# The token product of the remainder rows in four quarters of the array instead of two halves

## The chip, the core and the metric

One NeuronCore of a Trainium2 chip runs the whole program. The metric is the device time of one execution in microseconds (us). A core has a matrix engine (TensorE, PE in the profile, with its weight loads listed as PEld), a vector engine (VectorE, DVE), a scalar engine (ScalarE, ACT), GpSimd (POOL), a queue for DMA issues (SyncE, SP) and 16 DMA engines. TensorE is an array of 128 rows by 128 columns: a weight block ("stationary", `lhsT`) is loaded into it, and a second operand ("moving", `rhs`) is streamed through. An instruction may use a part of the array only: the partitions of its operands choose the rows, the partitions of its output in PSUM choose the columns. A profile shows that as `64*128` (64 rows by 128 columns), `128*64` or `64*64`.

## The reference, cut to what matters

Attention without softmax, with an RMS norm, feeds an MLP mixer. All is fp32.

```python
kv = np.einsum('bhsd,bhse->bhde', k, v)
out = np.einsum('bhsd,bhde->bhse', q, kv)
x = out / rms * g_norm                      # (8, 8, 576, 64) -> x (8, 576, 512)
xt = x.transpose(0, 2, 1)
h = np.maximum(xt @ w_tok1, 0.0) @ w_tok2   # w_tok1 (576, 256), w_tok2 (256, 576)
u = x + h.transpose(0, 2, 1)
h2 = np.maximum(u @ w_ch1, 0.0) @ w_ch2     # w_ch1 (512, 1536), w_ch2 (1536, 512)
return u + h2
```

The change is in `xt @ w_tok1`, the first token product. Its sum runs over 576 sequence rows, four blocks of 128 and a remainder of 64.

## The kernel before, in words

The eight batches go in four pairs. For a pair, attention makes the rows x: `X[pair, c]` for c from 0 to 3 holds 128-row blocks, two each, the first four blocks for the pair's first batch and the next four for its second; `X[pair, 4]` holds the two remainders together, those of the first batch on partitions 0 to 63 and those of the second on 64 to 127 (`x_of(pair, 8)`). `w_tok1r` holds the 64 remainder rows of the token weights twice, on both partition halves. The weights come as 64-bit words that ACT and DVE decode into fp32: four ACT steps a block (lines 183 to 201), then three DVE steps (lines 204 to 213); this decoding of the channel weights runs beside the token mixing, one block after another.

Token mixing (`token_mixing`, line 611) has these steps for a pair:

- `h` followed by side and t (`tok1`, line 614): for each side (batch of the pair) and each half t of the 256 token channels, a sum over four 128-row blocks in a PSUM bank `acc[side, t]` of 128 partitions by 512. These use the whole array.
- `hr` (`tok1_rem`, line 621): the 64 remainder rows are added to all four banks. Side 0 uses array rows 0 to 63, side 1 rows 64 to 127; both have all 128 columns. Then four `relu` on ACT (line 130) copy the banks to `h1` in SBUF, which frees the banks.
- `z` (`seed`, line 632): ACT copies x into a PSUM bank ahead of a later product.
- `u0` to `u8` (`tok2`, line 638): the second token product, read from `h1`, in order; `u8` makes the remainder rows of both batches in two column halves of the array (`128*64`).

Attention has `kv` (line 399; from pair 1 on in column halves, `128*64`), `kr` (`kv_rem`, line 417; the remainder rows, in quarters, `64*64`) and, from pair 1 on, `a` (`attend`, line 465), also in quarters, with 64 moving columns.

Every instruction goes through a helper that keeps the program's order (`matmul` line 135, shown as L136; `relu` L130; `copy` L133; `tensor_add` L127; `dma` L124). The order is written by hand as lists of step names that `play` (line 1334) runs: `middle` (line 1398), the two lists of `steady` (line 1404) and `last` (line 1456). In `middle`, `hr` of pair 0 follows `kv01 kr0 e00 e01` of pair 1's attention and is followed by `a0`. In both lists of `steady`, `hr` (of pairs 1 and 2) follows `h11` and is followed by `a1` of the next pair's attention. In `last`, `hr` (of pair 3) follows `h11`, and `u0` comes next. On ACT, the four `relu` come after the decoding steps that the lists put ahead of `hr`, and ahead of the `z` copy.

PSUM has two banks tagged `o`, two `kv` and four `h` (line 97). `acc` takes the four `h` banks; the `z2` seed and then `u0` of pairs 0 to 2 take the first ones that the `relu` free. `u0` and `u1` of pair 3 take `o` banks.

After the four pairs come the channel products (`channel1_once` and on), from 182 us to the end: long runs of whole-array matmuls of 256 columns, with DVE sums around them.

Of the kernel before, what the change touches and what calls it, by code (L numbers as in the profile page):

```python
# [20 lines left out]
def kernel(  # L21
# [33 lines left out]
    P = 128  # L55
# [5 lines left out]
    J, JJ, HF, Q = 4, 5, 64, 32  # L61
# [41 lines left out]
    w_tok1r = tokw.tile([P, DTOK], F32, name="w_tok1r")  # L103
# [11 lines left out]
    def do(f, *a, **kw):  # L115
        return lambda: f(*a, **kw)
# [6 lines left out]
    def dma(o, i, engine=nc.sync):  # L123
        keep(engine.dma_start(o, i))  # L124

    def tensor_add(o, a, b, op=ALU.add, engine=nc.vector):
        keep(engine.tensor_tensor(out=o, in0=a, in1=b, op=op))  # L127

    def relu(o, a):
        keep(nc.scalar.activation(o, a, AF.Relu))  # L130

    def copy(o, a):
        keep(nc.scalar.copy(o, a))  # L133

    def matmul(*a, **kw):
        keep(nc.tensor.matmul(*a, **kw))  # L136
# [248 lines left out]
    def x_of(pair, i):  # L385

        return X[pair, i // 2][:, i % 2]
# [223 lines left out]
    def token_mixing(pair, seeds, aside=()):  # L611
        h1, acc = {}, {}

        def tok1(side, t, js=range(J)):
            if js[0] == 0:
                acc[side, t] = ps["h"].tile([P, DM], F32, name="ps_h", tag="h")
            for j in js:
                matmul(acc[side, t], lhsT=w_tok1[j // 2][:, j % 2, ts(t, P)],
                                 rhs=x_of(pair, side * J + j), start=(j == 0), stop=False)

        def tok1_rem():
            for t in range(NTOK):
                for side in range(2):
                    r = ds(side * HF, HF)
                    matmul(acc[side, t], lhsT=w_tok1r[r, ts(t, P)],
                                     rhs=x_of(pair, 8)[r], start=False, stop=True)
            for side in range(2):
                h1[side] = hp_.tile([P, NTOK, DM], F32, name="h1", tag="h1")
                for t in range(NTOK):
                    relu(h1[side][:, t], acc[side, t])  # L630

        def seed(i):


            acc[i] = ps["h"].tile([P, DM], F32, name="ps_u", tag="h")
            copy(acc[i], x_of(pair, i))

        def tok2(i):
            if i not in seeds:
                n = "o" if i in aside else "h"  # L640
                acc[i] = ps[n].tile([P, DM], F32, name="ps_u", tag=n)
            first = i not in seeds
            if i < 8:
                for t in range(NTOK):
                    matmul(acc[i], lhsT=w_tok2[:, t, ts(i % J, P)], rhs=h1[i // J][:, t],
                           start=(first and t == 0), stop=(t == NTOK - 1), skip_group_check=True)
            else:
                for t in range(NTOK):
                    for side in range(2):
                        matmul(acc[i][ds(side * HF, HF)], lhsT=w_tok2[:, t, LO:],  # L650
                               rhs=h1[side][:, t],
                               start=(first and t == 0), stop=(t == NTOK - 1), skip_group_check=True)
            x = x_of(pair, i)
            if first:
                tensor_add(x, acc[i], x)
            else:
                copy(x, acc[i])
            if i == 8:
                dma(u_rest[ts(pair, P)], x, nc.gpsimd)
                for side in range(2):  # L660
                    dma(out[2 * pair + side, LO:], x[ds(side * HF, HF)], nc.gpsimd)
            elif i % 2 == 1:
                dma(
                    u_rows(2 * pair + i // J)[ds((i % J - 1) * P, 2 * P)]
                    .rearrange("(t p) e -> p t e", p=P), X[pair, i // 2], nc.gpsimd)

        steps = {f"h{s}{t}": do(tok1, s, t) for s in range(2) for t in range(NTOK)}
        steps |= {f"h{s}{t}{j}": do(tok1, s, t, (j,)) for s in range(2) for t in range(NTOK) for j in range(J)}
        steps |= {f"z{i}": do(seed, i) for i in seeds}
        return steps | {"hr": tok1_rem} | {f"u{i}": do(tok2, i) for i in range(9)}  # L670
# [714 lines left out]
    def spread_g():  # L1385
# [5 lines left out]
    start = [  # L1391
        "j21 zk00 zk01 ka00 ka01 gs kb00 e00 kb01 e01 eg0 eg1 l0 w01 w02 w03 w04 j4",
        "a00 q00 t00 m00 r00 i00", "a01 q01", "ag dg g01 t01 m01", "a10 q10", "a11 q11 r01 zk10 zk11 i01 w51 d01 w52 w53 w54",
        "w30 w40 lq0 h000 h010", "kv10 e10 g10", "kv11 e11 g11 t10 t11 m1 r1 i1 d10 w11 w12 w13 w14 l1", "h001", "h011", "a20 q20",
        "a21 q21 s11", "a30 q30", "a31", "h002 h012 g20 g21 t20 t21 m2 r2 i2 d20 g30 q31 s21 g31 t30",
        "a40", "h003 h013 t31 m3",
        "r3 i3 d30 q40 s31 g40 t40 m4 r4 w21 i4 d40 lr0 lr1"]
# [161 lines left out]
```

## Time and profile before

| | us |
|---|---|
| time, median of 3 runs | 768.65 (768.58 to 768.66) |
| time of the profiled execution | 768.43 |
| its span, first to last instruction | 766.6 |
| PE busy in the span | 761.2 |
| matmuls of the remainder rows, 32 instructions, mean of one | 0.59 |
| PE waits in all, longest | 2.1, 1.1 |

The span leaves out what lies around the program's instructions. A busy PE is a PE with a matmul in its pipeline: matmuls overlap, and the profile lists a 512-column matmul at 0.59 us although the next begins 0.43 later. Two matmuls that use different parts of the array begin almost together, some 7 ns apart. "x8" in a timeline counts instructions; an fp32 matmul of the source is two of them, each with its weight load.

### The profile page before, as it was taken

What the parts mean: (1) busy time and instruction counts of PE and PEld (TensorE: products, weight loads), DVE (VectorE), ACT (ScalarE), POOL (GpSimd) and SP (SyncE); (2) the same over time, 40 slices, a digit from 0 to 9 for tenths busy, and PEclk for the clock granted to TensorE, in tenths of its full rate; (3) what the DMA queues carried; (4) which work ended last, traced back from release to release, by engine and by line L of the source; (5) the groups of instructions that cost most, each with busy time, mean ns of one, the idle gap of its engine ahead of it and who ended that gap; (6) DMA issues with size and microseconds to landing.
All of it is one profiled execution on the core that took longest, in us unless ns stands there. A gap on an engine that the chain in (4) does not pass through costs nothing.

```text
span 766.6 us, 12767 instructions
## 1 busy us (share of the span) xinstructions
PE 761.2 (99%) x4694; PEld 613.0 (80%) x4694; DVE 644.5 (84%) x958; ACT 279.0 (36%) x563; POOL 110.8 (14%) x121
## 2 busy tenths in 40 slices
PE   9999999999999999999999999999999999999998
PEld 8655555446888888888888888888888888888887
DVE  3868896997757779899969889997898996798997
ACT  3656575773210232511234242123352223325211
POOL 0003030203410000002240002042000218000204
PEclk9999999999999999999999999999999999999999
DMA  9999999799799785589998578999649879845689
GB/s 353 325 331 375 318 380 329 252 319 350 252 289 321 288 283 170 175 270 216 216 231 246 157 214 227 261 187 264 202 145 293 166 225 205 209 147 152 153 203 121
DMA packets 138941, 188.28 MB, mean 246 GB/s; under 512 B 48896, under 2 KB 97536, under 8 KB 136832
## 3 DMA queue, kind: packets, MB, share of 16 engines
q1 hardware_dynamic: 103200, 168.72, 69.1%
q0 software_dynamic: 34848, 18.36, 16.0%
q8 instruction: 38, 0.62, 0.3%
q10 hardware_dynamic: 832, 0.39, 0.2%
q14 instruction: 23, 0.19, 0.1%
HBM read 138.28 MB, written 49.15 MB: 244 GB/s over the span
## 4 chain that ended last, share of the span: by engine, by line
PE 96%; DMA 2%; DVE 1%; SPq 0%; ACT 0%; issue 0%; DVEq 0%
PE ps_d L136 28%; PE ps_b L136 19%; PE ps_a L136 19%; PE ps_u L136 8%; PE ps_h L136 8%; PE ps_v L136 5%; PE ps_c L136 3%; PE ps_w L136 2%; PE ps_kv L136 2%; PE ps_o L136 2%; DMA raw<-in_moe_w_tok_dram 2%; DMA v_in<-in_v_dram 1%; PE ps_r L136 0%; DVE x L506 0%; DVE ms L534 0%; DVE w_tok L213 0%
## 5 line engine op out<-in xcount | busy, mean ns | idle before, releaser
L136 PE MATMUL ps_d<-ui,w 128*128 128x256 f32 x504 | 118.6, 379 | 0.0
L136 PEld LDWEIGHTS ps_d<-ui,w 128*128 128x128 f32 x504 | 95.8, 190 | 13.0
L133 ACT COPY ps_d<-ps_a 128x768 f32<-128x768 f32 (+1 forms) x56 | 32.0, 572 | 199.9 <-PE ps_a L136 196.9
L127 DVE TENSOR_TENSOR v<-v,v 128x1536 f32<-128x1536 f32 (+2 forms) x70 | 103.3, 1483 | 0.3
L136 PE MATMUL ps_b<-sv,w 128*128 128x256 f32 x324 | 78.9, 379 | 0.0
L136 PE MATMUL ps_a<-v,w 128*128 128x256 f32 x324 | 78.7, 379 | 0.0
L1288 POOL DMA_DIRECT2D out_dram<-us x24 | 26.8, 1836 | 291.8 <-ACT p L133 286.5
L136 PEld LDWEIGHTS ps_b<-sv,w 128*128 128x128 f32 x324 | 61.2, 190 | 8.9 <-issue 0.6
L136 PEld LDWEIGHTS ps_a<-v,w 128*128 128x128 f32 x324 | 61.6, 190 | 8.4
L136 PE MATMUL ps_u<-h,w_tok 128*128 128x512 f32 (+1 forms) x160 | 64.7, 599 | 0.0
L130 ACT ACTIVATE v<-v 128x768 f32<-128x768 f32 (+1 forms) x54 | 42.7, 822 | 55.1 <-DVE v L127 50.7
L136 PE MATMUL ps_d<-v,w 128*128 128x256 f32 x258 | 62.7, 379 | 0.0
L136 PE MATMUL ps_h<-x,w_tok 128*128 128x512 f32 x128 | 57.6, 600 | 0.7 <-DVE w_tok L213 0.6
L1288 POOL DMA_DIRECT2D out_dram<-r x40 | 41.3, 1926 | 102.0 <-ACT p L133 80.3
L136 PE MATMUL ps_d<-sv,w 128*128 128x256 f32 x228 | 55.4, 379 | 0.0
L136 PEld LDWEIGHTS ps_d<-v,w 128*128 128x128 f32 x258 | 49.0, 190 | 6.6
L136 PEld LDWEIGHTS ps_u<-h,w_tok 128*128 128x128 f32 (+1 forms) x160 | 25.6, 179 | 31.1 <-issue 27.0
L136 PEld LDWEIGHTS ps_d<-sv,w 128*128 128x128 f32 x228 | 43.3, 190 | 5.9
L136 PE MATMUL ps_a<-uT,w 128*128 128x256 f32 x192 | 46.7, 379 | 0.0
L136 PEld LDWEIGHTS ps_h<-x,w_tok 128*128 128x128 f32 x128 | 23.5, 190 | 28.3 <-issue 24.2
L136 PE MATMUL ps_b<-ui,w 128*128 128x256 f32 x168 | 40.8, 379 | 0.0
L136 PEld LDWEIGHTS ps_a<-uT,w 128*128 128x128 f32 x192 | 36.5, 190 | 5.0
(176 smaller groups left out, 1294.7 us busy)
## 6 DMA issues: line engine op xcount, KB each, us to landing
w<-parts SPq DMA_DIRECT2D x168, 384.0 KB
w<-parts SPq DMA_DIRECT2D x56, 192.0 KB
uT<-blocks SPq DMA_DIRECT2D x36, 256.0 KB
k_in<-in_k_dram SPq DMA_DIRECT2D x8, 1024.0 KB
v_in<-in_v_dram SPq DMA_DIRECT2D x8, 1024.0 KB
qT<-in_q_dram SPq DMA_DIRECT2D x8, 1024.0 KB
out_dram<-x POOLq DMA_DIRECT2D x16, 512.0 KB, 6.8
raw<-in_moe_w_ch_dram SPq DMA_DIRECT2D x8, 768.0 KB
```

The costliest lines, as they stand in the source:

```text
L127: keep(engine.tensor_tensor(out=o, in0=a, in1=b, op=op))
L130: keep(nc.scalar.activation(o, a, AF.Relu))
L133: keep(nc.scalar.copy(o, a))
L136: keep(nc.tensor.matmul(*a, **kw))
L1288: keep(nc.gpsimd.dma_start(to, t()[ds(b * Q, Q), at].rearrange("p n l j -> p n (l j)"), accum_op=ALU.add))
```

## The change

The product of the remainder rows is cut once more: for each t and each side, the 128 token channels are taken as two column halves n, so that an instruction uses 64 rows by 64 columns of the array, and (n, side) name the four quarters. The columns streamed and the sums are the same; 16 instructions stand where 8 stood, for each of the four pairs. The first four blocks now carry the stop flag on their fourth matmul, and the remainder's matmuls go on adding to the banks after it (`start=False`); the group check of the language is switched off for both.

```diff
                 matmul(acc[side, t], lhsT=w_tok1[j // 2][:, j % 2, ts(t, P)],
-                                 rhs=x_of(pair, side * J + j), start=(j == 0), stop=False)
+                                 rhs=x_of(pair, side * J + j), start=(j == 0), stop=(j == J - 1), skip_group_check=True)
 
         def tok1_rem():
             for t in range(NTOK):
-                for side in range(2):
-                    r = ds(side * HF, HF)
-                    matmul(acc[side, t], lhsT=w_tok1r[r, ts(t, P)],
-                                     rhs=x_of(pair, 8)[r], start=False, stop=True)
+                for n in range(2):
+                    for side in range(2):
+                        r = ds(side * HF, HF)
+                        matmul(acc[side, t][ds(n * HF, HF)], lhsT=w_tok1r[r, ds(t * P + n * HF, HF)],
+                               rhs=x_of(pair, 8)[r], start=False, stop=True, skip_group_check=True)
             for side in range(2):
```

## The prediction

> **What bounds the kernel now.** I read the page first: busy shares and the chain of waits.
>
> ```profile
> PE 761.2 (99%) x4694; PEld 613.0 (80%) x4694; DVE 644.5 (84%) x958; ACT 279.0 (36%) x563; POOL 110.8 (14%) x121
> PE 96%; DMA 2%; DVE 1%; SPq 0%; ACT 0%; issue 0%; DVEq 0%
> ```
>
> TensorE carries 96% of the chain that ended last, and the table of waits has PE waiting 2.1 us in all, every wait within the first 42 us. So a microsecond less of TensorE work is a microsecond less of span, as long as what TensorE reads is there that much earlier. The granted clock is 1.00 in every stretch. Two questions follow: what the four remainder products (`hr`) cost, and whether their inputs and their readers can follow.
>
> Next the timeline of PE (start, length, engine, shape, count). Lengths overlap, since matmuls are pipelined, so I work with differences of starts.
>
> ```profile
> 42.06 0.46 PE L136 MATMUL ps_kv<-v_in,k_in 64*64 64x64 f32 x16
> 42.45 1.99 PE L136 MATMUL ps_h<-x,w_tok1r 64*128 64x512 f32 x8
> 44.37 1.16 PE L136 MATMUL ps_o<-kvp,qT 64*64 64x64 f32 x64
> 45.46 1.12 PE L136 MATMUL ps_u<-h,w_tok 128*128 128x512 f32 x2
> ...
> 66.92 1.89 PE L136 MATMUL ps_u<-h,w_tok 128*64 128x512 f32 x8
> 68.74 0.46 PE L136 MATMUL ps_kv<-v_in,k_in 64*64 64x64 f32 x16
> 69.02 1.11 PE L136 MATMUL ps_o<-kvp,qT 64*64 64x64 f32 x64
> 70.06 0.70 PE L136 MATMUL ps_h<-x,w_tok 128*128 128x512 f32 x1
> ...
> 148.87 1.94 PE L136 MATMUL ps_u<-h,w_tok 128*64 128x512 f32 x8
> 150.73 0.70 PE L136 MATMUL ps_h<-x,w_tok 128*128 128x512 f32 x1
> ```
>
> Each fp32 matmul of the source is two instructions, so `hr` is 8: four groups of two that run side by side (row halves). All four `hr` take 1.92 from their start to the next product's: 42.45 to 44.37, 85.28 to 87.20, 126.67 to 128.58, 164.66 to 166.58. The weight loads give the pitch of the groups:
>
> ```profile
> 85.82 0.19 PEld L136 LDWEIGHTS ps_h<-x,w_tok1r 64*128 64x128 f32 x2 [0.24 <-issue]
> 86.25 0.19 PEld L136 LDWEIGHTS ps_h<-x,w_tok1r 64*128 64x128 f32 x2 [0.24 <-issue]
> ```
>
> A group of 512 columns takes 0.43; four take 1.72. The remaining 0.20 is the **change of shape**: on entering, the first weight load is not hidden (85.28 to 85.82 is 0.54, so 0.10 or 0.11 more than 0.43); on leaving, about 0.09 passes before the next shape starts.
>
> **What the change does, and its price.** `hr` becomes 16 instructions of 64\*64: four groups of four. Columns streamed per group stay 512. What is removed is changes of shape, where the neighbour already is 64\*64.
>
> Pitch of four quarters at 512 columns: the trace has no such instruction. Nearest rows: the 64\*64 products of `attend` run four side by side, 64 instructions in 69.02 to 70.06 = 1.04, or 0.065 a group for 64 columns, and the column halves of `u8` run two side by side at 512 columns, with 128 rows each, in 0.43 a group (66.92 to 68.74 = 1.82 = 4 x 0.43 and an exit of 0.10). That pair already streams as many rows times columns as four quarters would. Bounds: 0.43 (all four together) and 0.86 (two at a time). I take 0.43.
>
> Price of entering and leaving, from pairs of rows of the same work:
> - Entering 64\*64 from another shape: 64 `attend` products take 1.09 (44.37 to 45.46) against 1.04 after a product of the same shape (69.02): 0.05.
> - Leaving 64\*64: the 16 `kr` products take 0.39 when `hr` of another shape follows (42.06 to 42.45), 0.28 when `attend` follows (68.74 to 69.02): 0.11.
> - 512 columns with 64-column weights, entered from another shape: `u8` takes 1.86 at 148.87 against 1.82 at 66.92: 0.05 with rounding, where 128-column weights pay 0.10.
>
> By pair:
> - Pair 0 (`kr0`, `hr`, `a0`; all would be 64\*64): now 0.39 + 1.92 + 1.09 = 3.40; then 0.28 + 1.72 + 1.04 = 3.04. Saved 0.36.
> - Pairs 1 and 2 (`h11` 128\*128, `hr`, then `a1` or `a1` of the next play, 64\*64): now 1.92 + 1.09 = 3.01; then 0.05 + 1.72 + 1.04 = 2.81. Saved 0.20 each.
> - Pair 3 (128\*128 on both sides): now 1.92; then 0.05 + 1.72 + 0.11 = 1.88. Saved 0.04 or 0.05.
>
> TensorE's own sum: 0.36 + 0.20 + 0.20 + 0.05 = **0.81 us**. The 32 added matmuls and 32 added weight loads (eight of each a product) lie beside the streaming of 0.43 a group; without that cover each pair would cost about what one `attend` product does, 1.04/64 = 0.016, together 0.5. The changed start and stop flags of `tok1` add no instruction, and no DMA, queue or wait is moved: `relu` still waits for the last matmul of its sum.
>
> The Trainium skill has a rule that speaks against this (TensorEngine Tiling (Array Packing), Performance Considerations, Instruction Overhead): each matmul carries about 60 cycles of overhead, so a tiling factor is not worth having where the instructions are already small. As an estimate from that page, with the 2.4 GHz of TensorE: Matmul & The Clock Gate (Part 1), 32 more instructions would be 0.8 us, and the sum would be nothing. The trace disagrees for 64\*64: 0.016 us an instruction is less than 60 such cycles, 0.025.
>
> **What of it reaches the end.** `u0` follows `hr` and reads h1, which four `relu` on ACT make. Where ACT is tied to something else than TensorE, an earlier `hr` buys a wait. The timeline of ACT:
>
> ```profile
> 127.95 1.23 ACT L198 ACTIVATE w_ch<-raw 128x512 f32<-128x512 f32 x2 [1.73 <-DMA raw<-in_moe_w_ch_dram]
> 129.21 1.25 ACT L201 ACTIVATE raw<-raw 128x512 uint32<-128x512 uint32 x2
> 130.35 2.05 ACT L130 ACTIVATE h<-ps_h 128x512 f32<-128x512 f32 x4
> ...
> 163.27 1.26 ACT L198 ACTIVATE w_ch<-raw 128x512 f32<-128x512 f32 x2 [2.07 <-DMA raw<-in_moe_w_ch_dram]
> 164.56 1.27 ACT L201 ACTIVATE raw<-raw 128x512 uint32<-128x512 uint32 x2
> 165.82 0.60 ACT L130 ACTIVATE h<-ps_h 128x512 f32<-128x512 f32 x1
> ```
>
> Twice the `relu` stand behind four decoding steps that were started by a landing weight DMA. From 100 to 128 us the DMA engines are 97% busy or more, and SP's own waits up to 128 us are mostly for landings, so I take these landings as fixed.
> - Pair 2: `relu` step by (2.05 - 0.60)/3 = 0.48, so the second, which frees the bank that `u0` writes, ends at 130.35 + 0.48 + 0.60 = 131.43. With 0.07 for the release (estimate: about twice the 0.04 by which the `relu` at 165.82 follows the end of its matmul) `u0` can start at 131.50. It starts at 132.08 now: 0.58 of room, and TensorE would come 0.36 + 0.20 + 0.20 = 0.76 earlier. 0.18 is lost.
> - Pair 3: the same four decoding steps end so that `relu` can follow 1.14 after the second pair starts (129.21 to 130.35), here at 165.70 instead of 165.82. It ends at 166.30, and `u0` can start at 166.37 instead of 166.58. **Only 0.21 passes**; TensorE, 0.63 early by then, would stand for 0.42.
> - Pairs 0 and 1 have cover: pair 0's second `relu` follows its matmuls and ends 0.4 before `u0`; pair 1's ends at 87.10 + 1.08 = 88.2, 2.5 before `u0` at 90.70.
>
> Behind pair 3 the order is unchanged. The gain that is left, 0.21, is taken to the end.
>
> The sum against the profiled execution: its span is 766.6, its time 768.43, so 1.8 lies around the span; the median is 768.65, 0.2 above. Less 0.21: span 766.4, median 768.44.
>
> **Rivals.**
> - **All of it passes** (0.81; 767.84): if ACT's decoding moves with TensorE, because the landings were themselves released by something earlier. For: SP waited 18.7 us in 128 to 200 us for DVE to free raw buffers, and DVE and ACT take some of their work from TensorE. Against: both landings end idle time of ACT, and the first falls in the DMA-bound stretch.
> - **Nothing is gained** (768.65): the pause is tied to a change of operands, not of shape, or the added instructions cost about what is saved. Against: at 68.74 to 69.02 and 66.92 operands change without a pause; 32 times 0.016 is 0.5, not 0.81.
> - **Slower: the quarters don't run four at a time at 512 columns.** Place: all four products; the moving rows of each half are read twice, by two quarters. Price if they go two by two: 16 groups x 0.43 = 6.9, less 0.8, so 774.7. It decides from 0.81/16 = 0.05 more a group, a pitch of 0.48. For: no row of this trace shows four at 512 columns. Against: `attend` also reads each row half twice and runs at 0.065 a group; `u8` streams as much at 0.43.
>
> The skill's 60 cycles would put the time at no change too, in the second rival.
>
> **Chances.** Forecast (0.1 to 0.4 gained) 0.50; all of it 0.27; nothing, or a few tenths lost to a new wait 0.15; slower by the quarters or a chain of new waits 0.06; more than 1.5 gained, for which I see no mechanism, 0.02. What a measurement of this kernel can tell from no change is about 0.2%, 1.54 us; the first three all lie within it: faster 0.02, same 0.92, slower 0.06. The forecast is 768.4, its own range 768.2 to 768.6. The full range reaches from all of it with 0.2 for other executions, 767.6, to a few tenths lost, 769.1.
>
> **What would show it.** Right: `ps_h<-x,w_tok1r` 64\*64 x64, group pitch 0.43; `kr0` to `a0`'s end in 3.04; `hr` to the next start 1.72 in pair 0, 1.77 in pairs 1 and 2, 1.88 in pair 3; `u0` of pair 3 waits for ACT about 0.4, with the decoding before it at an unchanged 163.3. Wrong: a pitch above 0.48 (slower); no wait at that `u0` and the decoding earlier by as much as TensorE (all of it passes); a new wait after 182 us.

## The result, and the profile after

The changed kernel took 767.49 us (median of 22 executions) against 768.65 for the kernel before: ratio 0.9984, 95% interval 0.9977 to 0.9991, or 0.7 to 1.8 us less. The 1.16 between the medians is 0.15%, inside the 0.2% named in the prediction; the time lies a little beyond the low end of its range (767.6), and the gain is more than the 0.21 that it let pass. Two later sets of the same comparison gave 0.9987 (0.9978 to 0.9996) and 1.0001 (0.9992 to 1.0009), so the first set shows the most of the three. Over the three, the medians of all executions are 767.65 (44) and 768.51 (70), 0.86 apart.

TensorE's timeline after the change (start, length, engine, shape, count), at pair 0, pair 1 and pair 3:

```profile
42.14 1.90 PE L136 MATMUL ps_h<-x,w_tok1r 64*64 64x512 f32 x16
43.86 1.11 PE L136 MATMUL ps_o<-kvp,qT 64*64 64x64 f32 x64
44.90 1.55 PE L136 MATMUL ps_u<-h,w_tok 128*128 128x512 f32 x3
...
84.56 1.95 PE L136 MATMUL ps_h<-x,w_tok1r 64*64 64x512 f32 x16
86.33 1.11 PE L136 MATMUL ps_o<-kvp,qT 64*64 64x64 f32 x64
87.37 1.21 PE L136 MATMUL ps_kv<-v_in,k_in 128*64 128x64 f32 x34
...
163.53 1.95 PE L136 MATMUL ps_h<-x,w_tok1r 64*64 64x512 f32 x16
165.41 2.84 PE L136 MATMUL ps_u<-h,w_tok 128*128 128x512 f32 x6
```

Read the differences of starts: `hr` takes 1.72 in pair 0 (1.92 before), 1.77 in pair 1, 1.88 in pair 3, and `a0` and `a1` 1.04 (1.09 before). These are the prediction's four numbers. `kr0` starts at 41.86, so `kr0` to the end of `a0` takes 3.04, as predicted. The weight loads give the pitch of four quarters at 512 columns, which no row of before had:

```profile
85.04 0.15 PEld L136 LDWEIGHTS ps_h<-x,w_tok1r 64*64 64x64 f32 x4 [0.28 <-issue]
85.47 0.15 PEld L136 LDWEIGHTS ps_h<-x,w_tok1r 64*64 64x64 f32 x4 [0.28 <-issue]
```

It is 0.43, as for two halves: four quarters run together, and the 32 added matmuls lie beside the streaming. On ACT, ahead of pair 3's `relu`:

```profile
161.79 1.26 ACT L198 ACTIVATE w_ch<-raw 128x512 f32<-128x512 f32 x2 [2.74 <-DMA raw<-in_moe_w_ch_dram]
163.07 1.26 ACT L201 ACTIVATE raw<-raw 128x512 uint32<-128x512 uint32 x2
164.67 0.60 ACT L130 ACTIVATE h<-ps_h 128x512 f32<-128x512 f32 x1 [0.34 <-PE ps_h L136]
```

The decoding is still started by a landing, but at 161.79, not at 163.27. ACT then sits idle 0.34 until the matmuls end, and `u0` follows `hr` without a wait. The span is 765.3 (766.6 before): TensorE's last matmul starts 1.17 earlier. Comparing the starts of every run of matmuls in the two profiles, the steps are 0.20 before 42 us, 0.36, 0.20, 0.20 and 0.04 in the four products, and 0.16 in pair 0's `ps_r` at 59 us. The first and last of these lie outside the change.

### The profile page after: what moved, and what is told of

It is laid out like the page before. It is cut to its first block, busy times and chain, and to the rows that moved or that the text cites. A ratio compares the mean times of both kernels' runs of the same rounds, so it can differ in the third digit from the quotient of the medians.

```text
span 765.3 us, 12834 instructions
## 1 busy us (share of the span) xinstructions
PE 760.5 (99%) x4726; PEld 613.9 (80%) x4726; DVE 644.5 (84%) x958; ACT 279.0 (36%) x563; POOL 110.8 (14%) x121
## 4 chain that ended last, share of the span: by engine, by line
PE 96%; DMA 2%; DVE 1%; SPq 0%; ACT 0%; issue 0%; DVEq 0%
PE ps_d L136 28%; PE ps_b L136 19%; PE ps_a L136 19%; PE ps_u L136 8%; PE ps_h L136 8%; PE ps_v L136 5%; PE ps_c L136 3%; PE ps_w L136 2%; PE ps_kv L136 2%; PE ps_o L136 2%; DMA raw<-in_moe_w_tok_dram 1%; DMA v_in<-in_k_dram 1%; PE ps_r L136 0%; DVE x L506 0%; DVE ms L534 0%; DVE w_tok L213 0%
```

## The experiments

After the result, three theories stood. A: TensorE's 0.80 passes whole, and the rest of the first difference is loads that happened to arrive otherwise. B, the prediction's: the landings ahead of the `relu` are fixed and let only a part pass. C: the change also removes the waits at the start and at 59 us. Each run below is also read by the steps of TensorE's starts against the first profile of before; "elsewhere" is the sum of all steps between 42 us and TensorE's last matmul outside the products, good to about 0.02. A plus sign means earlier than in that profile.

| run | set's ratio to before (interval) | start, to 42 us | `hr` of pairs 0, 1, 2, 3 | elsewhere |
|---|---|---|---|---|
| first, changed | 0.9984 (0.9977 to 0.9991) | +0.20 | 0.36, 0.20, 0.20, 0.04 | +0.16 |
| e1, changed again | 0.9987 (0.9978 to 0.9996) | -0.02 | 0.36, 0.20, 0.20, 0.04 | +0.03 |
| e12, changed, third | 1.0001 (0.9992 to 1.0009) | +0.07 | 0.36, 0.20, 0.20, see text | -1.24 with pair 3 |
| e2, before again | 1.0002 (0.9993 to 1.0011) | +0.32 | 0 | -0.18 |
| e3, pair 0 only | 1.0006 (0.9997 to 1.0015) | +0.22 | 0.36, 0, 0, 0 | +0.16 |
| e10, e11, pair 0 only | one execution each | +0.25, +0.11 | 0.36, 0, 0, 0 | -0.44, +0.16 |
| e4, pairs 1 to 3 | 0.9991 (0.9982 to 1.0000) | +0.14 | 0, 0.20, 0.20, 0.04 | -1.27 |

**The same kernels again.** e1 and e12 are the changed kernel, e2 the kernel before.

> The changed kernel once more. Theory A (shape, all passes): the starts of TensorE's matmuls give the same 0.36, 0.20, 0.20 and 0.04 us less in the four remainder products (0.80 in all), no wait of TensorE at u0 of pair 3, and what the first profile showed beyond that (0.20 before 28 us, 0.16 in pair 0's attention at 59 us) is the arrival of loads and comes out another way here. Theory B (fixed landings, the prediction): the early decoding in the first profile was luck; here the decoding before pair 3's relu lands near 163 us, and u0 waits 0.1 to 0.5. Theory C (the change also takes away those two waits): both are gone again, and the time is 1.1 to 1.3 below before.

> The kernel before once more, as a control. A and B: the ratio to before holds 1; the start and the 0.16 at 59 us differ from its first profile. C: the 0.16 at 59 us is there again, and the first matmul of the token product again starts near 27.98 us.

> The changed kernel a third time. Theory A: 0.80 in the four products, whatever the waits for loads around them; ratio to before 0.9985 to 0.9992. If the gain is less than 0.2% here, as in the two sets before, 0.8 us is its size, and what is above it is the loads' arrival.

e1 came out as A says: 0.80 in the products, next to nothing elsewhere, 767.61 against 768.49. In e2 the start differs by 0.32 from the first profile of the same code and the wait at 59 us is 0.20 longer; in e1 it is there again in part. So C falls: these waits come and go with the execution, on unchanged code too. e12 has the same products, but its set holds 1, outside what A had asked for. Its profiled execution (768.74) lost time in three places, 0.32 at 59 us (the profile names no cause), 0.26 before pair 1's `hr` and 0.40 at 137 us (there TensorE waits for the queries' load), and then in B's place:

```profile
163.91 1.25 ACT L198 ACTIVATE w_ch<-raw 128x512 f32<-128x512 f32 x2 [2.90 <-DMA blocks<-w_ch]
165.19 1.28 ACT L201 ACTIVATE raw<-raw 128x512 uint32<-128x512 uint32 x2
166.37 2.03 ACT L130 ACTIVATE h<-ps_h 128x512 f32<-128x512 f32 x4
```

```profile
164.81 1.95 PE L136 MATMUL ps_h<-x,w_tok1r 64*64 64x512 f32 x16
167.00 1.55 PE L136 MATMUL ps_u<-h,w_tok 128*128 128x512 f32 x3 [0.24 <-ACT h L130]
```

The decoding began at 163.91, and here the profile names the write-out `blocks<-w_ch` as the DMA that ended its wait, not the load. The four `relu` run back to back behind it without waiting for TensorE, and `u0` starts 2.19 after `hr` instead of 1.88. Theory B's wait exists, in this execution.

**Parts of the change.** e3, e10 and e11 keep the quarters in pair 0 only, e4 in pairs 1 to 3 only:

```diff
-                for n in range(2):
+                m = HF if pair == 0 else P        # e4: HF if pair > 0 else P
+                for n in range(P // m):
                     for side in range(2):
                         r = ds(side * HF, HF)
-                        matmul(acc[side, t][ds(n * HF, HF)], lhsT=w_tok1r[r, ds(t * P + n * HF, HF)],
+                        matmul(acc[side, t][ds(n * m, m)], lhsT=w_tok1r[r, ds(t * P + n * m, m)],
```

> Quarters in pair 0 alone, halves in pairs 1 to 3. A: 0.36 less from kr0 to the end of a0, nothing in the other products (1.92 each), time 0.3 to 0.4 below before. B: 0.36 there, but about 0.15 of it comes back as a wait at u0 of pair 3. C: the wait at 59 us is gone here too, as it lies behind pair 0's product: 0.5 or more below before.

> Quarters in pairs 1 to 3, halves in pair 0. A: 0.20, 0.20 and 0.04 less, 0.44 in all, time 0.4 to 0.5 below before. B: 0.2 at most passes pair 3. C: the wait at 59 us is there as before, since nothing ahead of it has changed.

> Quarters in pair 0 alone, a second profile, for the executions that took 769.0 to 770.2 where others took 767.8 to 768.2. If a late landing between 68 and 73 us is what costs 1 us: a slow execution shows TensorE waiting 0.5 to 2 us at pair 1's h11 near 80 us behind ACT's scaling of x, with the decoding ahead of it starting after 71 us. If it comes from the start: the wait lies before 42 us, and the products after it keep their distances.

> Quarters in pair 0 alone, a third profile; expected as in the second one. In a fast execution (768.3 or less) no wait above 0.4 after 42 us.

The products add up pair by pair, to the hundredth. The times do not follow as neatly. e4's set is 0.47 below before, as A has it, though its interval (0 to 1.4) can't tell that from B's 0.2. Its profile is of a longer execution (769.02) with one wait of 0.99 at 80 us:

```profile
78.36 1.98 PE L136 MATMUL ps_h<-x,w_tok 128*128 128x512 f32 x4
81.07 2.41 PE L136 MATMUL ps_h<-x,w_tok 128*128 128x512 f32 x5 [0.73 <-ACT x L569]
```

The tile of x that `h11` reads was scaled late, since a decoding ahead of it on ACT waited for a landing until 72.05 (70.22 in the profile of before, 69.68 in the changed kernel's). e3's set is not faster: four executions at 767.8 to 768.2, seven at 769.0 to 770.2. The three profiles of this kernel (e3, e10, e11) are of executions of 767.8 to 768.3, so what makes the others longer was not seen. e10 shows B's wait a second time, with the halves in pair 3:

```profile
163.34 1.25 ACT L198 ACTIVATE w_ch<-raw 128x512 f32<-128x512 f32 x2 [3.09 <-DMA raw<-in_moe_w_ch_dram]
164.62 1.25 ACT L201 ACTIVATE raw<-raw 128x512 uint32<-128x512 uint32 x2
165.78 2.03 ACT L130 ACTIVATE h<-ps_h 128x512 f32<-128x512 f32 x4
```

```profile
163.88 1.99 PE L136 MATMUL ps_h<-x,w_tok1r 64*128 64x512 f32 x8
166.40 1.98 PE L136 MATMUL ps_u<-h,w_tok 128*128 128x512 f32 x4 [0.53 <-ACT h L130]
```

The landing is at 163.34, near the one in the profile of before; TensorE was 0.78 early, and 0.18 was left of it. The prediction had 0.21 for such a landing.

**The change of shape by itself.** e7 puts a product of the whole array, with zeros as its moving columns, between the quarters and what follows them (cut: the tile of zeros is left out):

```diff
+            if pair < 3:
+                matmul(acc[0, 0][:, :HF], lhsT=ones, rhs=zeros, start=False, stop=True, skip_group_check=True)
             for side in range(2):
                 h1[side] = hp_.tile([P, NTOK, DM], F32, name="h1", tag="h1")
```

> The changed kernel with one product of the whole array (128*128, 64 columns of zeros, added to the bank of side 0, t 0) behind hr in pairs 0 to 2, so that the quarters do not stand next to a_n in the same shape. If the gain is the change of shape: leaving 64*64 0.11, a first load of 128 columns 0.10, two instructions of 0.06, leaving 0.09, entering 64*64 0.05: 0.40 to 0.45 a pair, 1.2 to 1.35 in all, so 0.4 to 0.5 above before. If a pause only follows the operands or their number: the two instructions alone, 0.12 a pair, 0.36 in all, still 0.4 below before.

```profile
42.32 1.90 PE L136 MATMUL ps_h<-x,w_tok1r 64*64 64x512 f32 x16
44.15 0.43 PE L136 MATMUL ps_h<-zeros,ones 128*128 128x64 f32 x2
44.51 1.16 PE L136 MATMUL ps_o<-kvp,qT 64*64 64x64 f32 x64
45.75 0.70 PE L136 MATMUL ps_u<-h,w_tok 128*128 128x512 f32 x1
```

From `hr` to `a0` there are now 2.19 (1.72 in the changed kernel), 0.47 for two instructions of 64 columns; `a0` pays its entry again. In pair 1 the two together cost 0.52. Without the changes of shape the two instructions would be about 0.12 (an estimate: a group of 64 columns follows the one before it after 0.058 in `attend`). In pair 0, `u0` also waits 0.15, because `relu` waits for the added product. The set took 769.05 against 768.49, 1.0007 (0.9999 to 1.0016), 0.56 above before where 0.4 to 0.5 was expected; the interval takes in no change, so it is the trace that carries this. There three times 0.52 and the 0.15, less the 0.80, make 0.9. A pause for new operands alone, expected at 0.12 a pair, is ruled out by the 0.52. The added product brings a new shape and new operands at once, and the same product in 64\*64 was not run; but in the changed kernel's pair 0, `kr0`, `hr` and `a0` follow one another in one shape with different operands and show no pause (0.28, 1.72 and 1.04). The pause follows the shape.

**The place of the decoding.** e5 puts the decoding step that stands ahead of the `relu` of pairs 2 and 3 behind them; e6 puts one more ahead of those of pair 3:

```diff
-"h11 f10 1 1", "hr z2",              ->  "h11 f10 1", "hr z2 1",              (e5, pair 2)
-"h11 2 o2", "hr z2 1 o4",            ->  "h11 1 o2", "hr z2 2 o4",            (e5, pair 3)
-"h11 2 o2", "hr z2 1 o4", "u0 z3 1 c0", "u1 z4 1 c1 o5"
+"h11 5 o2", "hr z2 o4", "u0 z3 c0", "u1 z4 c1 o5"                             (e6, pair 3)
```

> The changed kernel, with the decoding step that stood just ahead of the four relu of pairs 2 and 3 put behind them. Theory A (all of TensorE's 0.80 passes; u0 does not wait for a decoding): the same 0.36, 0.20, 0.20 and 0.04 in the products, no other step of TensorE's starts, time as the changed kernel, 0.8 to 1.0 below before. Theory B (the decoding holds u0 in part of the executions): 0.2 to 0.5 lower than the changed kernel.

> The changed kernel with three more rounding steps, and with them ACT's decoding of the last channel block, put ahead of the relu of pair 3. Theory B's mechanism made sure of: the relu then stand behind one more landing and 2.4 us of decoding, so u0 of pair 3 waits 1 to 3 us, and the time is 1 to 3 above the changed kernel. If ACT's place does not matter because relu run anyway in time: no wait at u0, time as the changed kernel.

e6 brings B's wait about for certain: the second decoding starts at 164.40, and

```profile
163.81 1.95 PE L136 MATMUL ps_h<-x,w_tok1r 64*64 64x512 f32 x16
167.47 1.98 PE L136 MATMUL ps_u<-h,w_tok 128*128 128x512 f32 x4 [1.72 <-ACT h L130]
```

TensorE waits 1.7. The set took 771.20 against 768.35, 1.0045 (1.0030 to 1.0060); its four executions spread from 769.2 to 773.2. From the decoding's start to `u0` there are 3.07 here, 3.06 in e10, 3.09 in e12; the prediction had 3.10 (163.27 to 166.37).

e5 shows that the wait can't be had for nothing: `u0` waits no more, but the decoding now stands ahead of the `z` copies, and TensorE waits for those (the line is of e5):

```profile
174.97 7.28 PE L136 MATMUL ps_u<-h,w_tok 128*128 128x512 f32 x20 [0.26 <-ACT ps_u L133]
```

0.56 is lost between 166 and 182 us, and the set, 768.21 against 768.49, 0.9997 (0.9988 to 1.0006), is no better than the changed kernel.

**Two attempts at a better version.** e8 puts `kr1` next to `a1`, with the start flag on it; e9 puts the second channel block's decoding behind the scaling of x, against the wait seen in e4 (cut: for e8, the lines that move the start flag and the banks' allocation are left out):

```diff
-"a1 q10 g11 q11 g10", "kv10 kv11 kr1 e10 e11 t10 t11 m0 r0"
+"a1 q10 g11 q11 g10", "kr1 kv10 kv11 e10 e11 t10 t11 m0 r0"                   (e8, in both lists)
-            if n + 1 < len(blocks):
+            if 0 < n < len(blocks) - 1:                                       (e9, in stream)
-            steps += [clamp, shift, add]
+            steps += [clamp, shift, add] + [blocks[1][1]] * (n == 0)
-"h00 -i3 -d31 -s30 l0 b00 1 1", ... "h10 t00 t01 b01 x10 1", "h11 1 x11 1"
+"h00 -i3 -d31 -s30 l0 b00 1", ... "h10 t00 t01 b01 x10 1 1", "h11 1 x11 1 1"
```

> The changed kernel, with kr1 (64*64) put ahead of kv1 (128*64) in the attention of pairs 2 and 3, next to a1 (64*64), so that a change of shape each goes away. If changes of shape cost what the profile of before shows: 0.15 less each, 0.30 in all, 1.1 below before. If the remainder rows land too late for that place: TensorE waits there, and the time is above the changed kernel.

> The changed kernel, with the decoding of the second channel block (started by a landing between 68 and 72 us) put behind the scaling of x that pair 1's h11 reads, instead of ahead of attention's kvp copies. If late landings there are what costs about 1 us in some executions (0.99 at 80 us in the profile without pair 0): no such wait in the profile, a narrower spread, and a median 0 to 0.4 below the changed kernel. If the tail comes from elsewhere (the start): spread and median as the changed kernel.

e8: `a1` goes over into `kr1` without a pause, and 0.11 is saved there, but the first `kr1` products start one by one, for a reason that the profile does not name, and `kr1` takes 0.58 to `kv1`'s start where it takes 0.39 in the changed kernel. Net 0.08 is lost a pair, where 0.15 was to be gained; 767.76 against 768.49, 0.9992 (0.9984 to 1.0001). e9: no wait at 80 us in its profile, and an early scaling of x, but 0.32 more at 59 us, three of eleven executions still at 769.3 to 769.9, median 767.95, 0.9998 (0.9989 to 1.0007). Neither beats the changed kernel. With the decoding moved away from that place, e9 still has its longer executions; no profile shows where they lose their time.

## Why the prediction was right or wrong

**TensorE's sum** held to the hundredth: 0.36, 0.20, 0.20 and 0.04 in every profile of the changed kernel, 0.80 against the 0.81 predicted (in e12 the last 0.04 is hidden by the wait). So did each row it came from: leaving a shape, entering one, 0.43 for four quarters. That it is the shape and not the operands was argued from two rows; pair 0 of the changed kernel and e7 now bear it out. The rival of two quarters at a time is refuted by the pitch. That the 32 added instructions would eat the sum is refuted too: four quarters start some 7 ns apart and the group still takes 0.43. The rule of 60 cycles from the Trainium skill (TensorEngine Tiling (Array Packing), Instruction Overhead), taken as a cost added for every instruction, is not borne out here.

**What failed** is the step "I take these landings as fixed", and with it "Only 0.21 passes". The reason given, DMA engines 97% busy from 100 to 128 us, does not reach the load of pair 3, and a row that the prediction counted for the rival speaks of it: of the 18.7 us that SP waited for DVE to free raw buffers, 11.5 were ahead of this very load. Counted through in program order, the block decoded from 163.27 on is loaded by these two DMAs; the first pair of lines is of before, the second of the changed kernel:

```profile
148.34 2.08 DVE L213 CUSTOM_DVE_ANT_1 w_ch<-w_ch,raw 128x2048 uint16<-128x2048 uint16 x1
150.49 1.36 SPq L124 DMA_DIRECT2D raw<-in_moe_w_ch_dram  x2
...
146.22 2.08 DVE L213 CUSTOM_DVE_ANT_1 w_ch<-w_ch,raw 128x2048 uint16<-128x2048 uint16 x1
148.36 0.82 SPq L124 DMA_DIRECT2D raw<-in_moe_w_ch_dram  x2
```

The DVE step (L213) is the last of a block's decoding and frees its raw buffer. In all 14 profiles SP issues this load 0.06 to 0.07 after that step ends. So the landing is released by something earlier, as the rival had it, and is not fixed. It also scatters: in the eight profiles of before, the changed kernel and pair 0 only, the DVE step ends between 148.3 and 150.4, and the decoding begins 11.5 to 13.8 after the issue. It waits for the load and for the write-out `blocks<-w_ch`, and the profile names now one and now the other as the last.

The two `relu` behind a decoding were read from one execution, whose 163.27 was among the late ones: in the changed kernel's and the pair-0 profiles the decoding ahead of pair 3's `relu` began at 160.4, 160.6, 161.6, 161.8, 163.3 and 163.9, and in a second profile of before at 162.2. With the first four `u0` had no wait, and all that TensorE had gained passed pair 3; with the last two it came 0.60 and 0.31 later. The arithmetic of the wait was right (`u0` comes 3.1 after the decoding begins); its condition was a draw, not a constant. In four of these six the outcome was that of the rival "all of it passes", 767.84, to which 0.27 was given. Two profiles of before and three of the changed kernel are too few to tell whether the decoding also comes earlier on the whole because TensorE does.

**The size.** Against that rival the first set gave 0.35 more and the third 0.6 less. The three sets differ from before by 1.16, 0.88 and 0.22, each with an interval of about 0.7 to either side; together, 0.86, they agree with 0.80 but do not measure it closely. In the first profile the steps outside the products (start 0.20, 59 us 0.16) make up what goes beyond 0.80. They differ by as much on unchanged code (e2: 0.32 and 0.20), so that part of the first result was luck. They have no term in the prediction, and the range's low end allowed 0.2 for them.

**The prediction's cover in pairs 0 and 1** held: `u0` had 0.2 and more left behind the second `relu` in every profile of the changed kernel. Pair 2's loss of 0.18 was not seen: the second `relu` ended 0.6 to 1.6 before `u0`. The decoding ahead of it began at 125.8, 126.4 and 127.7 in the changed kernel's profiles, not at the 127.95 taken as fixed.

Open: what makes seven of eleven executions of e3 about 1 us slower, and by what rule the DVE step and the time from issue to decoding move between executions. No profile caught the first.

## What to carry to other kernels

When a product uses another part of the array than its neighbours, count the changes of shape in the matmul starts: here each exit cost about 0.1 us and each entry 0.05 to 0.10, and cutting a product further so that it matches its neighbours was free, as the quarters ran four at a time. A wait that depends on a landing should be priced from several profiles of the unchanged kernel, not from one, and what released the load should be looked up first. A gain of 0.1% on TensorE can be read exactly in the trace and hardly in the times, whose sets here differed by more than the gain.

## What the runs showed of the hardware that was not expected

- Decoding steps that wait for DMA began 2 to 3 us apart in executions of one program: at 67.6 to 71.1 us for the second channel block and at 161.6 to 163.9 for the later one, in three profiles of the changed kernel.
- The pause on leaving a shape hardly depends on the shapes: 0.08 to 0.11 from 128\*128, 128\*64, 64\*128 and 64\*64. The entry does: 0.10 with weights of 128 columns, 0.05 with 64. (For leaving the whole array: `h11` of pair 1 takes 7.06, where 16 instructions at 0.43 take 6.88; with an entry of 0.10, some 0.08 is left.)
- Two instructions of another shape in between cost 0.52 us, some four times the 0.12 estimated for their streaming.
